# Attention steps of two neighbouring units issued together, and the r-k products in one PSUM bank

## Chip, cores and metric

One core of one Trainium2 chip. The metric is the device time of one execution in microseconds (us); below, times without a unit are in us. The kernel before takes 1027.44 as the median of 3 runs (1026.24 to 1029.26).

## The reference

A decaying linear attention with a state, then two feed-forward layers over all 3072 tokens, all in float32.

```python
# r, k, v, w: (4, 8, 768, 48); u: (8, 48)
for t in range(S):
    cur = np.einsum('bhd,bhe->bhde', u[None] * kt, vt)
    y[:, :, t] = np.einsum('bhd,bhde->bhe', rt, state + cur)
    state = wt[:, :, :, None] * state + np.einsum('bhd,bhe->bhde', kt, vt)
x = y.transpose(0, 2, 1, 3).reshape(3072, 384)
h = x @ w_in                                   # (3072, 2048)
g = np.where(h >= 1, h, np.where(h <= -1, 0.0, (h + 1) ** 2 / 4))
x = g @ w_out                                  # (3072, 384)
g = x @ w_gate; val = x @ w_val                # (3072, 1536) each
out = (g * sigmoid(g) * val) @ w_out2          # (3072, 384)
```

## The kernel before, in words

**Attention** is cut into 24 units: 128 time steps of one batch with its 8 heads. A unit works in two chunks of 64 steps (c = 0, 1) and in four pairs of heads (e = 0, 1 within a pair; the second head of a pair lies from partition 64 on). Fourteen short steps make a unit, each a function `slot_...` with a letter in the table `PLAN`:

- `w`, `i`, `r`, `k`: bring w, r and k into the layout with the head dimension on partitions, make the running products of the decay (G and F), and scale r and k by them. For the first ten units the turning is done by TensorE (four transposes of L234 each, into a bank of PSUM); from unit `UD = 10` on VectorE does it (L217) from data loaded in blocks.
- `a` (`slot_a`, L318): the r-k products, 16 matmuls of 48x64 by 48x64 (L323), for the heads e = 0 and e = 1 in turn; ScalarE copies the two halves out (L332), GpSimd masks them (L333). `n` (L354): four transposes of the scaled k (L359), copied out by ScalarE (L363). `c` (L304): copies of r by ScalarE (L307), r*k*u by GpSimd (L310, L311), the next loads of r and k, and the carried state by VectorE (L289).
- `v` (L338): row sums and their product with v; ScalarE's copies of the carried state (L299). `q` (L366): 16 or 8 matmuls k-v (L373). `s` (L381): the state (L388, L289, L393). `t` (L296): copies by ScalarE (L299).
- `b` (L395): 16 matmuls of 112x64 by 112x48 that give the outputs (L399); VectorE adds (L407); three loads for the unit after next are issued (L185, L179).
- `y` (L416): three transposes of the outputs (L423) and ScalarE's copy `xh` (L426). `x` (L429): VectorE's rest `xl` (L431).

**The feed-forward layers** run as steps (phase, block, i). Phase 1 has 6 blocks of 4 units with 16 steps i each: `front1` is nine matmuls of 128x512 (L521; six with xh, three with xl) followed by ScalarE (L542, L543) and VectorE (L549); `split_act` makes gh (ScalarE L530) and gl (GpSimd L531); `back1` is nine matmuls (L559) of step i-2, since a list `pend` holds two steps back. Nine such matmuls are called a set below. Phase 2 has 6 blocks of 12 steps (L521, L611) and no attention.

**The order of the work** on every engine is the order of the calls (`manual_schedule`). A lead-in list `LEADSEQ` does units 0 to 3 and the beginning of unit 4. After it, time is counted in ticks: unit `un` has its step `nm` at tick `16 * un + PLAN[nm]`. In each step of phase 1, `attn_to` is called twice, once behind `front1` and once behind `back1`, and issues all attention steps whose ticks have come; within a tick they go by unit, and within a unit by a list of letters. Over the 29 calls of one block the ticks advance by 64. The units 4 to 7 are done in block 0, whose x they are for block 1, and so on. So attention stands between sets of feed-forward matmuls, in TensorE's one queue.

**PSUM.** `at_bank` (L226) hands out banks in turn: seven in the lead-in, three afterwards (L719). Of the other five, two are for `front1` and three for `back1`. Whoever gets a bank writes it only when its last reader is done. A unit takes 7 banks (a 2, n 1, q 2, b 1, y 1), and 3 more for w, r and k up to unit 9.

**Weights** arrive as float64. `conv_tick` (L481) turns one chunk of them into two float32r parts with ScalarE (L52 to L54, L495), VectorE (L59, L493, L496) and GpSimd (L489, L496). 9 ticks of it are in the lead-in, 26 in block 0, and two in block 1 that find the queue empty. `open_blk` (L191) then gives the memory of that stage to the block loads of r, k and w.

Of the kernel before, what the change touches and what calls it, by code (L numbers as in the profile page):

```python
# [16 lines left out]
ACTF = mybir.ActivationFunctionType  # L17
# [5 lines left out]
BLOCKS = [4] * 6  # L23

PLAN = {
    "w": 0, "i": 3, "r": 6, "k": 9, "c": 12, "a": 15, "n": 15, "v": 17, "q": 18, "s": 18, "t": 20, "b": 23, "y": 28,
    "x": 30,
}
FILL0 = 5
SKEW = 3  # L30
# [32 lines left out]
def rwkv_ffn_ffn_kernel(  # L63
# [14 lines left out]
    nc = tc.nc  # L78
# [6 lines left out]
    C = 64  # L85
# [5 lines left out]
    NU = NT * B  # L91

    starts = [sum(BLOCKS[:j]) for j in range(len(BLOCKS))]
    blk_of = {s + i: (j, i) for j, s in enumerate(starts) for i in range(BLOCKS[j])}
    NB1 = len(BLOCKS)
# [130 lines left out]
    def at_bank():  # L226
        t = at_b[bn[0] % len(at_b)]
        bn[0] += 1
        return t
# [87 lines left out]

    def slot_a(un):  # L318
        K, R = st[un]["K"], st[un]["R"]
        ab = [at_bank(), at_bank()]  # L320
        for f in range(2 * NP):
            for e in range(2):
                nc.tensor.matmul(  # L323
                    out=ab[e][0:C, f * C:(f + 1) * C],
                    lhsT=K[C * e:C * e + D, f, :],
                    rhs=R[C * e:C * e + D, f, :],
                    start=True,
                    stop=True,
                )
        for e in range(2):  # L330
            At = W[0:C, e]
            nc.scalar.activation(out=At, in_=ab[e][0:C].rearrange("q (f c) -> q f c", c=C), func=ACTF.Copy)  # L332
            nc.gpsimd.affine_select(  # L333
                out=At, in_=At, compare_op=ALU.is_ge, fill=0.0, base=-1,
                pattern=[[0, 2 * NP], [1, C]], channel_multiplier=-1,
            )
# [102 lines left out]
    at_tick = {}  # L439
# [3 lines left out]
    ticks = [0]  # L443
    led = set()

    def tick_of(un):

        return 16 * un + PLAN["x"] + 1

    def attn_to(t):  # L450
        while ticks[0] < t:
            for un, nm in sorted(at_tick.get(ticks[0], []), key=lambda z: (z[0], "wirkcanvqstbyx".index(z[1]))):
                if (un, nm) not in led:
                    stages[nm](un)
            ticks[0] += 1
# [17 lines left out]
    def conv_queue(src, slot, lo_eng):  # L473
        cq.append([src, slot, lo_eng, None])
# [34 lines left out]
    def cols(src, i):  # L509
        return src[:, 2 * i * P:2 * (i + 1) * P]  # L510

    def rows(src, i):
        return src[i * P:(i + 1) * P, :]
# [173 lines left out]
    with tc.manual_schedule():  # L687
        order = [(w_in, i) for i in range(SKEW)]
        for i in range(NF1):
            order += [(w_out, i)] + [(w_in, i + SKEW)] * (i + SKEW < NF1)  # L690
        for c, (src, i) in enumerate(order):
            part, slot = (cols(src, i), ws[2 * i]) if src is w_in else (rows(src, i), ws[2 * i + 1])
            conv_queue(part, slot, nc.vector if c in LOV else nc.gpsimd)
        for what in INIT:
            if what[0] == "n":
                load_nat(int(what[2]), what[1])
            elif what[0] == "v":
                load_v(int(what[1]))
            elif what[0] == "s":
                load_vs(int(what[1]), int(what[2]))  # L700
            elif what[0] == "u":
                nc.sync.dma_start(
                    out=u_b.rearrange("p h d -> p (h d)"), in_=u.rearrange("h d -> (h d)").partition_broadcast(P)
                )
            elif what[0] == "W":
                conv_load(int(what[1]))
        consts()

        for item in LEADSEQ:
            if item == "C":  # L710
                conv_tick()
            elif item[0] == "+":
                keep_warm(int(item))
            else:
                un = int(item[1:])
                stages[item[0]](un)
                led.add((un, item[0]))
        ticks[0] = tick_of(BLOCKS[0] - 1)
        del at_b[3:]  # L719
        pend = []  # L720

        def more_conv(n):
            for _ in range(n):
                conv_tick()

        for n, (ph, j, i) in enumerate(steps):
            if (ph, j, i) == (1, 1, 2):
                open_blk()
            if ph == 1:
                t0 = tick_of(starts[j] + BLOCKS[j] - 1)  # L730
                t1 = tick_of(starts[j + 1] + BLOCKS[j + 1] - 1) if j + 1 < NB1 else t0
            src = (front1 if ph == 1 else front2)(j, i)
            if ph == 1:
                attn_to(min(t1, t0 + (t1 - t0) * (2 * i + 1) // (2 * NF1 - 3)))
                if j == 0 or (j == 1 and i < 2):
                    conv_tick()
            if (ph == 2 and j == 0) or (ph == 1 and j == NB1 - 1 and i > 0):
                more_conv(1)
            if ph == 1 and j == NB1 - 1 and i % 3 == 2:
                more_conv(1)  # L740
            if ph == 1 and j == NB1 - 1 and i in (5, 6, 7):
                split_x1(0, i - 5)
            if ph == 2 and j + 1 < NB2 and i in (6, 7, 8):
                split_x1(j + 1, i - 6)
            if ph == 2 and j in (1, 2) and i % 3 == 2:
                range_check(4 * (j - 1) + i // 3)
            if ph == 1:
                src = gate1(j, src)
            else:
                pend.append((ph, j, i, split_act(src, 512, nc.gpsimd)))  # L750
            if len(pend) > LAG - (ph == 1):
                p_, j_, i_, g_ = pend.pop(0)
                (back1 if p_ == 1 else back2)(j_, i_, g_)
            if ph == 1:
                attn_to(min(t1, t0 + (t1 - t0) * (2 * i + 2) // (2 * NF1 - 3)))
                if j == 0 and (i % 2 == 0 or i < 4):
                    conv_tick()
                pend.append((ph, j, i, split_act(src, BLOCKS[j] * P, nc.gpsimd)))
            if ph == 1 and j == NB1 - 1:
                if i == 0:  # L760
                    open_p2()
                    for c in range(3 * NF2):
                        conv_queue(chunk2(c), slot2(*divmod(c, 3)), (nc.gpsimd, nc.vector)[c % 2])
                    conv_load()
                if i == 1:
                    load_x1(0)
            if ph == 2:
                if j == 0:
                    more_conv(1)
                if j + 1 < NB2:  # L770
                    if i == 2:
                        load_x1(j + 1)
                if j in (1, 2) and i % 3 == 0:
                    range_load(4 * (j - 1) + i // 3)
        for p_, j_, i_, g_ in pend:
            back2(j_, i_, g_)
# [186 lines left out]
```

## Time and profile before

| | |
|---|---|
| median of 3 runs | 1027.44 us |
| profiled execution | 1025.06 us, of which the span from first to last instruction is 1023.1 us |
| busy: TensorE (PE) | 977.9 us, 96% of the span |
| busy: VectorE (DVE), ScalarE (ACT), GpSimd (POOL) | 512.0, 546.2, 464.2 us |
| granted TensorE clock, mean | 0.976 |
| chain that ended last | PE 85%, ACT 5%, DVE 4%, POOL 2% |

The page of the profile lists busy time by engine, 40 slices of the span, the chain that ended last, and groups of instructions by line. Busy time of TensorE counts the pipelined length of a matmul, so two starts are compared below where a duration matters. fp32 products show twice as many matmuls in the trace as the program issues (x32 for 16). In the tables of stretches, block 0 runs from 60.3 to 165.7 us, block 2 from 247.6 to 329.6 us.

### The profile page before, as it was taken

How to read it: one execution, taken by the hardware profiler on the slowest of the kernel's cores; microseconds unless marked ns; L12 is line 12 of the kernel's file. 1: busy time of each engine (PE TensorE's matmuls, PEld its weight loads, DVE VectorE, ACT ScalarE, POOL GpSimd, SP SyncE). 2: the span in 40 equal slices, each digit the busy share in tenths (PEclk: the TensorE clock that was granted, in tenths of full speed). 3: DMA queues.
4: the chain of work that ended last, by engine and by line, in shares of the span. 5: the costliest groups of instructions: out<-in, count | busy, mean ns of one | idle time of the engine just before them, and what ended most of it. 6: DMA issues, size and time to landing. Idle time of an engine off the chain costs nothing.

```text
span 1023.1 us, 16697 instructions
## 1 busy us (share of the span) xinstructions
PE 977.9 (96%) x6430; PEld 817.6 (80%) x6431; DVE 512.0 (50%) x779; ACT 546.2 (53%) x1016; POOL 464.2 (45%) x424
## 2 busy tenths in 40 slices
PE   6678879999999999999999999999999999999997
PEld 4556657888788788788877888888888888888886
DVE  7878866686776777675255663222221222222221
ACT  3678887565656655665699883334333221221211
POOL 4568776544454544454287775232232232232221
PEclk7789989999999999999999999999999999999999
DMA  9755531663455546450443540201200100100000
GB/s 172 168 136 144 142 99 32 161 115 82 109 119 99 121 85 122 98 104 1 130 134 123 178 139 1 85 24 47 86 24 24 62 1 1 62 1 1 31 1 34
DMA packets 164825, 84.33 MB, mean 82 GB/s; under 512 B 115457, under 2 KB 155522, under 8 KB 164738
## 3 DMA queue, kind: packets, MB, share of 16 engines
q1 hardware_dynamic: 164738, 83.19, 33.8%
q8 instruction: 52, 0.85, 0.4%
q14 instruction: 35, 0.29, 0.1%
HBM read 73.73 MB, written 9.44 MB: 81 GB/s over the span
## 4 chain that ended last, share of the span: by engine, by line
PE 85%; ACT 5%; DVE 4%; POOL 2%; issue 2%; SPq 1%; DMA 1%; ACTq 0%; POOLq 0%; DVEq 0%
PE bank L521 45%; PE bank L559 17%; PE bank L611 15%; PE bank L399 2%; PE bank L323 2%; PE bank L359 1%; PE bank L373 1%; DVE ws L496 1%; ACT a L542 1%; POOL t L489 1%; PE bank L234 1%; PE bank L423 1%; DVE F L263 1%; ACT n L53 1%; DVE G L253 1%
## 5 line engine op out<-in xcount | busy, mean ns | idle before, releaser
L531 POOL TENSOR_TENSOR gl<-a,gh 128x512 fp32r<-128x512 f32 x168 | 219.6, 1307 | 440.5 <-ACT gh L530 426.4
L521 PE MATMUL bank<-xh,ws 128*128 128x512 f32 x1332 | 346.7, 396 | 3.5 <-DVE a L549 3.4
L521 PEld LDWEIGHTS bank<-xh,ws 128*128 128x128 f32 x1332 | 246.5, 188 | 54.3 <-DVE a L549 6.0
L530 ACT ACTIVATE gh<-a 128x512 fp32r<-128x512 f32 x168 | 105.5, 628 | 156.7 <-DVE a L601 116.9
L521 PE MATMUL bank<-xl,ws 128*128 128x512 f32 x666 | 188.1, 390 | 0.0
L600 DVE TENSOR_TENSOR a<-a,bank 128x512 f32<-128x512 f32 x72 | 49.5, 687 | 266.5 <-ACT a L599 266.5
L559 PE MATMUL bank<-gh,ws 128*128 128x512 f32 x576 | 153.5, 402 | 0.0
L521 PEld LDWEIGHTS bank<-xl,ws 128*128 128x128 f32 x666 | 125.2, 188 | 27.3
L611 PE MATMUL bank<-ws,gh 128*128 128x384 f32 x528 | 135.0, 336 | 0.0
L599 ACT ACTIVATE a<-bank 128x512 f32<-128x512 f32 x72 | 42.9, 595 | 166.5 <-PE bank L521 166.4
L559 PEld LDWEIGHTS bank<-gh,ws 128*128 128x128 f32 x576 | 104.9, 189 | 22.0 <-ACT x L569 1.1
L542 ACT ACTIVATE a<-bank,half 128x512 f32<-128x512 f32 x96 | 65.5, 682 | 74.0 <-PE bank L521 73.5
L549 DVE SCALAR_TENSOR_TENSOR a<-bank,a 128x512 f32<-128x512 f32 x96 | 65.5, 683 | 71.8 <-ACT a L543 59.7
L611 PEld LDWEIGHTS bank<-ws,gh 128*128 128x128 f32 x528 | 97.0, 188 | 5.0
L611 PE MATMUL bank<-ws,gl 128*128 128x384 f32 x264 | 89.0, 337 | 0.0
L559 PE MATMUL bank<-gl,ws 128*128 128x512 f32 x288 | 81.4, 391 | 0.0
L489 POOL TENSOR_TENSOR t<-t,n 128x384 int32<-128x384 int32 x68 | 76.3, 1124 | 0.4 <-DVE t L59 0.4
L601 DVE TENSOR_TENSOR a<-a,bank 128x512 f32<-128x512 f32 x72 | 49.5, 687 | 44.0 <-PE bank L521 43.3
L559 PEld LDWEIGHTS bank<-gl,ws 128*128 128x128 f32 x288 | 54.0, 188 | 11.8
L543 ACT ACTIVATE a<-a 128x512 f32<-128x512 f32 x96 | 60.7, 632 | 3.1
L59 DVE TENSOR_SCALAR t<-t 128x384 int32<-128x384 int32 x68 | 46.5, 685 | 15.6 <-ACT t L52 15.6
L611 PEld LDWEIGHTS bank<-ws,gl 128*128 128x128 f32 x264 | 49.5, 188 | 0.0
(108 smaller groups left out, 1165.9 us busy)
## 6 DMA issues: line engine op xcount, KB each, us to landing
raw<-in_moe_w_out_dram SPq DMA_DIRECT2D x28, 384.0 KB, 3.7
raw<-in_moe_w_in_dram SPq DMA_DIRECT2D x16, 384.0 KB, 4.2
bw<-in_w_dram SPq DMA_DIRECT2D x56, 96.0 KB, 2.9
br<-in_r_dram SPq DMA_DIRECT2D x56, 96.0 KB, 2.3
bk<-in_k_dram SPq DMA_DIRECT2D x56, 96.0 KB, 3.4
v<-in_v_dram SPq DMA_DIRECT2D x24, 192.0 KB, 3.7
V<-in_v_dram SPq DMA_DIRECT2D x48, 96.0 KB, 3.3
x_d<-x SPq DMA_DIRECT2D x18, 256.0 KB, 2.1
```

What stands on the lines that cost most here:

```text
L59: nc.vector.tensor_scalar(out=t, in0=t, scalar1=3, scalar2=None, op0=ALU.logical_shift_left)
L489: nc.gpsimd.tensor_tensor(out=f, in0=f, in1=three["n"], op=ALU.add)
L521: nc.tensor.matmul(out=bk[:, :n], lhsT=a[:, kk, :], rhs=b[:, kk, :n], start=(i == 0), stop=(i == 3 * KD - 1))
L530: nc.scalar.activation(out=gh[:, :n], in_=src[:, :n], func=ACTF.Copy)
L531: eng.tensor_tensor(out=gl[:, :n], in0=src[:, :n], in1=gh[:, :n].bitcast(F32), op=ALU.subtract)
L542: nc.scalar.activation(out=a[:, :n], in_=bk[:, :n], func=ACTF.Relu, scale=0.5, bias=half)
L543: nc.scalar.activation(out=a[:, :n], in_=a[:, :n], func=ACTF.Square)
L549: nc.vector.scalar_tensor_tensor(out=a[:, :n], in0=bk[:, :n], scalar=1.0, in1=a[:, :n], op0=ALU.max, op1=ALU.min)
L559: nc.tensor.matmul(out=acc_b[m][:, :n], lhsT=a[:, m * P:(m + 1) * P], rhs=b[:, :n], start=(i == 0 and s == 0), stop=(i == NF1 - 1 and s == 2),
L600: nc.vector.tensor_tensor(out=a, in0=a, in1=gb, op=ALU.mult)
L601: nc.vector.tensor_tensor(out=a, in0=a, in1=vb, op=ALU.mult)
L611: nc.tensor.matmul(out=bk[:, :DM], lhsT=a[:, t * P:(t + 1) * P], rhs=slot[:, b], start=(i == 0 and s == 0), stop=(i == NF2 - 1 and s == 2),)
```

## The change

`PLAN` moves steps to later ticks. Of unit un, `b` (tick 31) now falls on the tick of `a` and `n` of unit un+1 (31), and `y` (37) on that of `q` and `s` of unit un+1 (37); `c` comes after `a` and `n`. The r-k products of both heads of a pair go into one bank, those of e = 1 to partitions 64 to 127. A unit now takes 6 banks (9 up to unit 9). The ticks of block 0 go from 79 to 151 (72 of them; they went from 79 to 143), in the same 29 calls; the other blocks keep 64. `open_blk` is called two steps sooner, and the two empty ticks of `conv_tick` are gone. `LEADSEQ` is the same.

```diff
 PLAN = {
-    "w": 0, "i": 3, "r": 6, "k": 9, "c": 12, "a": 15, "n": 15, "v": 17, "q": 18, "s": 18, "t": 20, "b": 23, "y": 28,
-    "x": 30,
+    "w": 0, "i": 3, "r": 6, "k": 9, "a": 15, "n": 15, "c": 16, "v": 19, "q": 21, "s": 21, "t": 23, "b": 31, "y": 37,
+    "x": 38,
 }
...
-        ab = [at_bank(), at_bank()]
+        ps = at_bank()
...
-                    out=ab[e][0:C, f * C:(f + 1) * C],
+                    out=ps[C * e:C * (e + 1), f * C:(f + 1) * C],
...
-            nc.scalar.activation(out=At, in_=ab[e][0:C].rearrange("q (f c) -> q f c", c=C), func=ACTF.Copy)
+            nc.scalar.activation(out=At, in_=ps[C * e:C * (e + 1)].rearrange("q (f c) -> q f c", c=C), func=ACTF.Copy)
...
-        ticks[0] = tick_of(BLOCKS[0] - 1)
+        ticks[0] = 16 * BLOCKS[0] + PLAN["a"]
+        first = ticks[0]
...
-            if (ph, j, i) == (1, 1, 2):
+            if (ph, j, i) == (1, 1, 0):
                 open_blk()
             if ph == 1:
-                t0 = tick_of(starts[j] + BLOCKS[j] - 1)
-                t1 = tick_of(starts[j + 1] + BLOCKS[j + 1] - 1) if j + 1 < NB1 else t0
+                t0 = tick_of(starts[j] + BLOCKS[j] - 1) if j else first
+                t1 = tick_of(starts[j + 1] + BLOCKS[j + 1] - 1) if j + 1 < NB1 else tick_of(NU - 1)
...
-                if j == 0 or (j == 1 and i < 2):
+                if j == 0:
                     conv_tick()
```

The place in each block where outputs and r-k products stand, on TensorE. Before, in block 1 (L399 outputs, L423 their transposes, L323 r-k products, L359 transposes of k; bank_94 to bank_96 are attention's three):

```order
L399 MATMUL bank_96<-V_1_154,W 64x48
...
L521 MATMUL bank_92<-xh,ws_116 128x512 x6
L521 MATMUL bank_92<-xl,ws_116 128x512 x3
...
L423 MATMUL bank_94<-ident,rk 128x128 x3
L521 MATMUL bank_93<-xh,ws_118 128x512 x6
L521 MATMUL bank_93<-xl,ws_118 128x512 x3
L323 MATMUL bank_95<-F_148,K 64x64
L323 MATMUL bank_96<-F_148,K 64x64
...
L359 MATMUL bank_94<-ident,K 128x128 x4
L559 MATMUL bank_89<-gh,ws_115 128x512
```

Now, in block 1 as well:

```order
L521 MATMUL bank_92<-xl,ws_108 128x512 x3
L399 MATMUL bank_95<-V_0_153,W 64x48
...
L323 MATMUL bank_96<-F_149,K 64x64 x16
L359 MATMUL bank_94<-ident,K 128x128 x4
L559 MATMUL bank_89<-gh,ws_105 128x512
...
L521 MATMUL bank_93<-xl,ws_110 128x512 x3
L423 MATMUL bank_95<-ident,rk 128x128 x3
L373 MATMUL bank_96<-v,kt 48x48
L373 MATMUL bank_94<-v,kt 48x48
```

The outputs of one unit stand directly ahead of the r-k products of the next, and the transposes of the outputs directly ahead of the next unit's k-v products; each was a group between two sets of its own.

The same engine in block 0, where r, k and w are still turned by TensorE (L234; nr and nw are r and w). Before, the transposes of k take the bank of L423, and those of w one of the two banks of L323:

```order
L423 MATMUL bank_95<-ident,rk 128x128 x3
L559 MATMUL bank_89<-gh,ws_107 128x512
...
L323 MATMUL bank_96<-F_149,K 64x64
L323 MATMUL bank_94<-F_149,K 64x64
...
L359 MATMUL bank_95<-ident,K 128x128 x4
L521 MATMUL bank_92<-xh,ws_112 128x512 x6
L521 MATMUL bank_92<-xl,ws_112 128x512 x3
L234 MATMUL bank_96<-ident,nw_136 128x128 x4
```

Now:

```order
L423 MATMUL bank_96<-ident,rk 128x128 x3
L373 MATMUL bank_94<-v,kt 48x48
L373 MATMUL bank_95<-v,kt 48x48
...
L234 MATMUL bank_96<-ident,nr_138 128x128 x4
L521 MATMUL bank_93<-xh,ws_114 128x512 x6
```

The bank of L423 is next taken by the transposes of r, which stand behind the k-v products in the same group.

## Rows read from the trace of the kernel before

**Rows 1.** Stretches: length, busy (x count) of PE, PEld, DVE, ACT, POOL; clock, DMA share, GB/s.

```profile
60.30:165.70 105.40, 89.89 (x732) 69.91 (x731) 79.28 (x124) 88.92 (x177) 81.55 (x75) 0.95 0.49 127
247.60:329.60 82.00, 82.00 (x702) 65.79 (x701) 60.64 (x88) 50.51 (x91) 38.62 (x37) 1.00 0.51 107
```

**Rows 2.** Waits of PE: total us, times, longest; two of block 0, one from 170 us on.

```profile
PE bank L234 <- ACT W L332: 7.7, 3, 6.4
PE bank L359 <- DVE xl L431: 5.2, 2, 4.0
...
PE bank L521 <- DVE a L549: 2.4, 2, 1.7
```

**Rows 3.** Timeline of PE, block 2: start, length, line, operation; a and n, then q.

```profile
250.89 0.84 PE L521 MATMUL bank<-xl,ws 128*128 128x512 f32 x3
251.66 1.15 PE L323 MATMUL bank<-F,K 48*64 48x64 f32 x32
252.74 0.66 PE L359 MATMUL bank<-ident,K 128*128 128x128 f32 x4
...
254.62 0.86 PE L559 MATMUL bank<-gl,ws 128*128 128x512 f32 x3
255.41 0.58 PE L373 MATMUL bank<-v,kt 64*48 64x48 f32 x32
...
257.41 0.84 PE L521 MATMUL bank<-xl,ws 128*128 128x512 f32 x3
...
259.45 0.84 PE L559 MATMUL bank<-gl,ws 128*128 128x512 f32 x3
```

**Rows 4.** Timeline of PE, block 2: outputs b between two sets.

```profile
280.04 0.84 PE L559 MATMUL bank<-gl,ws 128*128 128x512 f32 x3
280.81 1.14 PE L399 MATMUL bank<-V,W 112*64 112x48 f32 x32
281.88 1.66 PE L521 MATMUL bank<-xh,ws 128*128 128x512 f32 x6
283.37 0.84 PE L521 MATMUL bank<-xl,ws 128*128 128x512 f32 x3
```

**Rows 5.** Timeline of PE, lead-in at the low clock: b directly ahead of a.

```profile
40.43 2.11 PE L399 MATMUL bank<-V,W 112*64 112x48 f32 x30 [3.41 <-ACT V L299]
42.47 1.97 PE L323 MATMUL bank<-F,K 48*64 48x64 f32 x32
```

**Rows 6.** Timeline of PE, block 0: transposes of r directly ahead of b.

```profile
121.31 0.85 PE L521 MATMUL bank<-xl,ws 128*128 128x512 f32 x3
122.00 0.60 PE L234 MATMUL bank<-ident,nr 128*128 128x128 f32 x4
122.52 1.14 PE L399 MATMUL bank<-V,W 112*64 112x48 f32 x32
...
125.08 0.85 PE L559 MATMUL bank<-gl,ws 128*128 128x512 f32 x3
```

**Rows 7.** Timeline, block 0: from the transposes y to the transposes of k.

```profile
78.96 0.50 PE L423 MATMUL bank<-ident,rk 128*128 128x128 f32 x3
...
85.41 0.47 ACT L426 ACTIVATE xh<-bank 128x384 fp32r<-128x384 f32 x1
...
86.75 1.11 PE L359 MATMUL bank<-ident,K 128*128 128x128 f32 x4 [3.98 <-DVE xl L431]
...
87.52 2.80 PE L521 MATMUL bank<-xh,ws 128*128 128x512 f32 x6
```

**Rows 8.** ACT's groups in block 0: busy us, mean ns, idle before.

```profile
L299 ACT ACTIVATE V<-m 48x192 f32<-48x192 f32 x16 | 5.8, 362 | 2.5 <-DVE m L289 2.2
L332 ACT ACTIVATE W<-bank 64x512 f32<-64x512 f32 x8 | 4.2, 576 | 0.0
L363 ACT ACTIVATE kt<-bank 128x384 f32<-128x384 f32 x4 | 1.9, 476 | 0.0
```

**Rows 9.** DMA issues of b's loads on the page: KB each, us to landing.

```profile
V<-in_v_dram SPq DMA_DIRECT2D x48, 96.0 KB, 3.3
```

More of the change, by code (lines that the diff above doesn't have):

```diff
@@ L451, in attn_to @@
         while ticks[0] < t:
-            for un, nm in sorted(at_tick.get(ticks[0], []), key=lambda z: (z[0], "wirkcanvqstbyx".index(z[1]))):
+            for un, nm in sorted(at_tick.get(ticks[0], []), key=lambda z: (z[0], "wirkancvqstbyx".index(z[1]))):
                 if (un, nm) not in led:
```

## The prediction

> **What bounds the kernel now.** I read the busy shares, then the table of stretches, then TensorE's waits, and last its timeline. The stretches show two kinds of time. In block 2 TensorE is busy for all of 82.00 us, while ScalarE has 50.51, VectorE 60.64 and GpSimd 38.62 [rows 1]; from 170 us to the end of attention it has no wait to speak of [rows 2]. There the time is the sum of what stands in TensorE's queue. Block 0 is different: of 105.40 us TensorE is busy 89.89, and the clock granted is 0.95; ScalarE is busy 88.92, the other two about 80 [rows 1], because the weights are converted there. Of the 15.5 us in which TensorE stands, 12.9 are two waits for a bank of attention: the transposes of w for ScalarE's copies of the r-k products (7.7), and those of k for the rest xl of the outputs (5.2) [rows 2]. The longest take 6.4 and 4.0. So a saving on TensorE counts in full behind block 0, and in block 0 the question is who waits for whom.
>
> **Prices on TensorE.** I compare the start of the last three matmuls of one set with that of the next set. With nothing between them this is 2.04 (257.41 to 259.45) [rows 3], or 0.227 a matmul. With a and n between them it is 3.73, so they cost 1.69; with q 2.79, so q costs 0.75 [rows 3]. With b it is 3.33, so b costs 1.29 [rows 4]. That 1.29 has three parts: 0.09 until it begins (0.77 less three matmuls, 0.68), 1.07 from its first product to the next set, and 0.13 by which the six first matmuls of that set are slow (1.49 for 1.36) [rows 4]. Products a also begin 0.09 late [rows 3].
>
> **Part 1: b directly ahead of a and n.** The restart of a set behind b (0.13) and the entry of a (0.09) go, if the step from b to a costs no more than that from b to a set. The lead-in shows that step at the low clock: 2.04 for 15 pairs of products and the step, 0.136 a pair [rows 5], against 1.07 for 16 pairs and the step to a set, 0.067 a pair, at the full clock [rows 4]. Twice the time at half the clock: the steps cost the same. So a join saves 0.22. Bounds: nothing, if the step eats it, and 0.31, if b's own 0.09 went too. There are 19 joins, 4 in block 0 and 15 behind it: 15 x 0.22 = **3.3 us** (0 to 4.7).
>
> **Part 2: y directly ahead of q.** Nearest row: transposes of r directly ahead of b. The two cost 3.77 - 2.04 = 1.73, that is b's 1.29 and 0.44 for four transposes [rows 6], 0.11 each, which is what a 128x128 transpose takes in the stream. Transposes and sets have the same shape on the array, so there was nothing to leave or enter in front of y, and the entry into q stays. I take 0 (0 to 0.09 each, the entry of a small product, 1.4 in all).
>
> **Part 3: eight ticks more in block 0.** Counted from the tables, block 0 takes over from later blocks a and n of unit 8, its q, and the transposes of w and r of unit 9: 1.69 + 0.75 + 2 x 0.44 = **3.3 us** less behind block 0. The last block gets no substitute.
>
> **Part 4: block 0 itself.** TensorE has 15.5 us free there, so its own 3.3 more is no price by itself. ScalarE has the longest work: unit 8 adds two copies L332, one L363 and two L299, 2 x 0.58 + 0.48 + 2 x 0.36 = 2.4 [rows 8]. If the engines hinder one another as much as before, the block gets 2.4 longer. The waits change places. The wait of k's transposes for xl goes: they now take the bank that k itself was read from, which a needs anyway. The wait of w for the copies L332 goes: its bank is now b's, read by VectorE. New is that the transposes of r take the bank of y, three times in the same group (behind q of units 5, 7 and 8), once a set later. They wait for ScalarE's xh and VectorE's xl. ScalarE ran late in this block: xh came 6.4 after y's transposes began [rows 7], and k's transposes could go 7.8 after them. So a new wait is at most 7.8 - 0.3 (y) - 0.75 (q) = 6.7, and, ScalarE being prompt, at least the 1.3 from xh's start to the release of the bank (85.41 to 86.75) [rows 7]; since VectorE has the three steps of s to do before xl, which wait for q (0.75), I call it 2. Three times 2 to 6.7 is 6 to 20, against the 12.9 that go. I take them as equal, for ScalarE's work sets the pace. After the 4.0 wait the next six matmuls took 2.80 [rows 7] where 1.66 is usual [rows 4], at the lower of the two clock levels; with shorter and more even waits I count one of the two such restarts as gone, 1.1. Block 0: 2.4 - 1.1 = **1.3 us longer** (from 5 shorter to 9 longer: waits of 2 or 6.7, 3.3 of work absorbed or not, both slow restarts gone or none).
>
> **Costed at nothing.** The products of a in one bank: 16 matmuls as before, still in pairs for e = 0 and e = 1; first and last pair start the same way. ScalarE's two copies read 64 partitions each as before. Clustered evacuation: where b, a, n and c fall into one call, ScalarE has the two L332, L363 and c's copies in a row ahead of gh, and GpSimd masks and multiplies ahead of gl. Since `back1` runs two steps behind, three sets (6.1) lie between the burst and the use of that gh; the delay is at most the burst, 1.29 + 1.69, and the 1.6 of L332 and L363, 4.6. If that cover were gone, some 1 or 2 us would be due at one place in each of four blocks. Queues: b's three loads leave 8 ticks later, about 10 us by 82.0 for 64 ticks [rows 1]; v is used 20 ticks (25 us) on and V 32, with 3.3 to landing [rows 9]. c's loads of r and k leave 4 ticks later and have 16 ticks. The block loads open two steps sooner, behind the last conversion, which stands in step 15 of block 0; GpSimd's three fills and SyncE's twelve issues wait there for nothing new. The lead-in has the same order and needs fewer banks: 0.
>
> **Sum.** 1025.06 (the profiled execution, span 1023.1) - 3.3 - 3.3 + 1.3 = 1019.8. The median is 2.38 above the profiled execution, so **1022.1** as a median. What 0.3% is, about all that a measurement here can tell from no change, is 3.1 us; the forecast is 5.3 faster.
>
> **A rule against the sum.** In the trace the pairs of a run two at a time: 16 pairs in 1.08 (251.66 to 252.74) [rows 3], with the two halves on different partitions of the input and in two banks. No row has two row halves of the array writing one bank at once; q, which does use all four quarters, sends each row half to a bank of its own. The Trainium skill, page "TensorEngine Tiling (Array Packing)", section Restrictions and Gotchas, says that different row tiles cannot access the same PSUM bank simultaneously. By that rule a's two halves would have to take turns; the sum above would be some 20 us higher.
>
> **Rivals.**
> - *The bank holds the halves apart (slower).* The mechanism is in a: pairs that shared 0.067 take turns, 1.08 becomes up to 2.16. 20 units behind the lead-in give up to 21.6, a part of the five in block 0 hidden: about 19, so 1041. It decides from the point where a is 0.27 longer, a quarter of its 1.08, since 20 x 0.27 is the whole 5.3. For it: the halves never shared a bank. Against it: b's pairs share one bank on different output partitions at 1.07 for 16 pairs [rows 4]; but there the halves are of columns. Chance 0.08.
> - *Block 0 eats it (no change).* The transposes of r meet a late ScalarE each time: 3 x 6.7 = 20 for 12.9, and the 3.3 of work is not absorbed. Block 0 grows by about 9; 1027.4 - 6.6 + 9 = 1030; with waits of 5 it is 1025. For it: xh was 6.4 late [rows 7]. Against it: TensorE's standing lets ScalarE catch up. Chance 0.17.
> - *Joining saves nothing.* The step from b to a drains like two. 1022.1 + 3.3 = 1025.4. For it: r ahead of b saved nothing [rows 6]. Against it: the lead-in's step. Chance 0.13.
> - *Block 0 gains.* The new waits are short (2 each) and the clock stays up: block 0 is 5 shorter, 1015.8. Chance 0.10.
>
> **How the numbers follow.** The forecast itself gets 0.45, with 1018 to 1024.3 of its own; 0.07 is left for what I don't see, mostly late gh and gl. Faster by over 0.3% (below 1024.4): 0.45 + 0.10 + 0.04 of the joins + 0.02 = 0.61. Within it: 0.09 of the joins + 0.11 of block 0 + 0.02 = 0.22. Slower (above 1030.5): 0.06 + 0.08 + 0.03 = 0.17. The range takes in the gain in block 0 with the upper bound of the joins (1014) and block 0 at its worst (1031); it leaves out the bank rival.
>
> **What would show it.** In the profile after: block 2 at about 81.1 instead of 82.0, and block 4 shorter by 3 or more; b, a and n between two sets at 2.76 (1.29 + 1.69 - 0.22); 16 pairs of a still in about 1.08; y and q together at about 1.1. In block 0: no wait of L359 for xl, none of L234 for L332, but L234 (nr) waiting for xl, two to four times. Wrong: a near 2 us; waits of L559 for gh or gl in blocks 1 to 4; a block 0 over 112 or under 99.

## The result, and where the time went

The changed kernel takes 1038.45 us as the median of 4 runs (1037.6 to 1039.22), beside 1027.47 for the kernel before: ratio 1.0109, 95% interval [1.0096, 1.0121]. It is slower by 11 us where 5 faster was forecast. The profiled execution took 1038.19, its span is 1036.2, the mean granted clock 0.972. All stretches, waits and timelines below come from one such execution of each kernel, while the executions of one kernel differ by up to 5 (1024.97 to 1029.77 in e11).

The table of stretches for the kernel after, blocks 0 to 4 (length, busy of PE, PEld, DVE, ACT, POOL, clock, DMA share, GB/s):

```profile
61.00:187.10 126.10, 96.41 (x808) 78.42 (x807) 87.86 (x133) 93.23 (x182) 87.96 (x78) 0.86 0.41 104
187.10:268.20 81.10, 81.10 (x705) 66.72 (x705) 59.88 (x87) 49.17 (x89) 44.40 (x39) 1.00 0.51 114
268.20:348.80 80.60, 80.60 (x702) 66.34 (x700) 62.40 (x88) 50.74 (x92) 44.61 (x36) 1.00 0.50 109
348.80:429.40 80.60, 80.60 (x686) 66.44 (x685) 61.78 (x87) 51.19 (x92) 44.57 (x36) 1.00 0.49 110
429.40:507.80 78.40, 78.40 (x586) 64.51 (x585) 44.90 (x61) 48.67 (x87) 37.04 (x32) 1.00 0.29 74
```

The same for the kernel before, blocks 1 and 4; blocks 0 and 2 are in [rows 1], and block 3 is as long as block 2:

```profile
165.80:249.60 83.80, 83.49 (x714) 67.14 (x713) 56.86 (x86) 51.75 (x94) 41.01 (x41) 1.00 0.49 105
...
413.70:495.70 82.00, 82.00 (x638) 65.84 (x637) 49.93 (x73) 49.33 (x89) 36.48 (x34) 1.00 0.34 77
```

Behind block 0 the change gains: block 1 is 2.7 shorter, blocks 2 and 3 are 1.4 shorter each and block 4 is 3.6 shorter, 9.1 in all. Block 0 loses 20.7 (105.40 to 126.10). The lead-in is 0.7 longer (61.00 for 60.30) and what follows block 4 1.0 longer, which I did not follow up. In block 0 TensorE stands for 29.7 (126.10 less 96.41) instead of 15.5, and is busy 6.5 longer: 3.3 of that, by the prediction's prices, is the work of eight more ticks, and the rest goes with the clock of 0.86 (it was 0.95). TensorE's waits in block 0 after the change (in total, times, longest) show where:

```profile
PE bank L234 <- DVE xl L431: 26.5, 4, 10.6
PE bank L234 <- DVE S L388: 1.8, 1, 1.8
```

The two waits of before [rows 2] are gone, as forecast, and four new ones have come, one at r of each of the units 6 to 9. (The wait for L388 is one more: k's transposes now take the first bank of q, which VectorE frees with the state.) The first in TensorE's timeline after:

```profile
85.34 0.60 PE L234 MATMUL bank<-ident,nw 128*128 128x128 f32 x4
...
89.91 0.49 PE L423 MATMUL bank<-ident,rk 128*128 128x128 f32 x3
90.33 0.58 PE L373 MATMUL bank<-v,kt 64*48 64x48 f32 x32
101.47 1.11 PE L234 MATMUL bank<-ident,nr 128*128 128x128 f32 x4 [10.57 <-DVE xl L431]
102.23 2.91 PE L521 MATMUL bank<-xh,ws 128*128 128x512 f32 x6
```

From the transposes of w (85.34) to those of r TensorE has two sets, y and q; it is done with them at 90.9 and stands for 10.57. The six matmuls after it run at the low clock level (granted clock 0.50), 2.91 for the usual 1.66 [rows 4]; so they do after each of the four (2.81 to 2.91), and after the wait for L388 (2.91). Meanwhile VectorE's timeline after has no idle time:

```profile
86.97 0.67 DVE L245 TENSOR_SCALAR F<-bank 128x512 f32<-128x512 f32 x1
...
87.67 3.88 DVE L253 TENSOR_TENSOR_SCAN G<-F,seed 128x520 f32<-128x520 f32 x1
91.48 1.09 DVE L59 TENSOR_SCALAR t<-t 128x384 int32<-128x384 int32 x1
92.49 1.35 DVE L496 TENSOR_TENSOR ws<-t,ws 128x384 fp32r<-128x384 f32 x1
...
94.45 1.61 DVE L263 TENSOR_TENSOR_SCAN F<-F,seed 128x520 f32<-128x520 f32 x1
...
99.75 0.34 DVE L388 TENSOR_TENSOR S<-bank,m 112x192 f32<-112x192 f32 x1
...
100.87 0.55 DVE L431 TENSOR_TENSOR xl<-bank,xh 128x384 fp32r<-128x384 f32 x1
```

This is the thing to see. Between VectorE's reading of w (L245, 86.97) and xl (100.87), which frees the bank that r wants, stand both scans of the decay of unit 6, whose r it is, five instructions of weight conversion (5.7), the row sums, a step of the feed-forward layer (L549) and the state, 13.2 in all. VectorE does them in the order of the program. In the kernel before, r's transposes took the bank of w, whose last reader is L245, ahead of all that.

VectorE is not the only late one. xl needs ScalarE's xh, and xh is late too. From the timelines of ScalarE and VectorE after, xh and xl of the four units (xl of the first is above):

```profile
96.27 0.46 ACT L426 ACTIVATE xh<-bank 128x384 fp32r<-128x384 f32 x1
...
124.04 0.46 ACT L426 ACTIVATE xh<-bank 128x384 fp32r<-128x384 f32 x1
126.51 0.55 DVE L431 TENSOR_TENSOR xl<-bank,xh 128x384 fp32r<-128x384 f32 x1
...
151.13 0.47 ACT L426 ACTIVATE xh<-bank 128x384 fp32r<-128x384 f32 x1
152.38 0.55 DVE L431 TENSOR_TENSOR xl<-bank,xh 128x384 fp32r<-128x384 f32 x1
...
174.82 0.47 ACT L426 ACTIVATE xh<-bank 128x384 fp32r<-128x384 f32 x1
177.12 0.55 DVE L431 TENSOR_TENSOR xl<-bank,xh 128x384 fp32r<-128x384 f32 x1
```

xh begins 6.4, 4.4, 5.1 and 3.8 behind y's transposes, and xl follows it by 4.6, 2.5, 1.3 and 2.3. Where VectorE was ready and stood for xh, xl followed by 0.5 (146.52 and 147.02 in the trace of e9), and r's transposes begin 0.6 behind xl. So, as an estimate from these rows with ScalarE's times as they are, the four waits would be 6.5, 2.2, 5.2 and 3.9 if VectorE had nothing ahead of xl: some 18 of the 26.5 go with xh, and VectorE's queue adds 8.6.

In the steady part the prices are as forecast. TensorE's timeline after, block 1, b with a and n, then y with q:

```profile
251.51 0.84 PE L559 MATMUL bank<-gl,ws 128*128 128x512 f32 x3
252.28 1.14 PE L399 MATMUL bank<-V,W 112*64 112x48 f32 x32
253.35 1.15 PE L323 MATMUL bank<-F,K 48*64 48x64 f32 x32
254.43 0.66 PE L359 MATMUL bank<-ident,K 128*128 128x128 f32 x4
...
256.31 0.86 PE L521 MATMUL bank<-xl,ws 128*128 128x512 f32 x3
...
260.41 0.84 PE L521 MATMUL bank<-xl,ws 128*128 128x512 f32 x3
261.09 0.49 PE L423 MATMUL bank<-ident,rk 128*128 128x128 f32 x3
261.51 0.57 PE L373 MATMUL bank<-v,kt 64*48 64x48 f32 x32
...
263.51 0.84 PE L559 MATMUL bank<-gl,ws 128*128 128x512 f32 x3
```

Set to set the first burst takes 4.80 (251.51 to 256.31), so b, a and n cost 4.80 - 2.04 = 2.76, and y with q 3.10 - 2.04 = 1.06. In the kernel before, y alone stood like this:

```profile
285.41 0.85 PE L559 MATMUL bank<-gl,ws 128*128 128x512 f32 x3
286.10 0.49 PE L423 MATMUL bank<-ident,rk 128*128 128x128 f32 x3
...
287.82 0.84 PE L521 MATMUL bank<-xl,ws 128*128 128x512 f32 x3
```

That is 2.41 - 2.04 = 0.37; with q's 0.75 it makes 1.12. So the second join saves 0.06 and the first 0.22: 1.1 a block of four units, of the 1.4 by which blocks 2 and 3 are shorter; the other 0.3 is not explained.

### The profile page after: what moved, and what is told of

Same layout as the page of the kernel before. It is cut to its first block, busy times and chain, and to the rows that moved or that the text cites. A ratio compares the mean times of both kernels' runs of the same rounds, so it can differ in the third digit from the quotient of the medians.

```text
span 1036.2 us, 16614 instructions
## 1 busy us (share of the span) xinstructions
PE 979.6 (95%) x6431; PEld 828.1 (80%) x6431; DVE 521.0 (50%) x779; ACT 549.7 (53%) x1016; POOL 486.0 (47%) x424
## 4 chain that ended last, share of the span: by engine, by line
PE 87%; DVE 7%; ACT 3%; SPq 1%; issue 1%; DMA 0%; POOL 0%; DVEq 0%; ACTq 0%
PE bank L521 46%; PE bank L559 18%; PE bank L611 15%; PE bank L399 3%; PE bank L323 2%; DVE F L263 1%; DVE G L253 1%; PE bank L359 1%; PE bank L234 1%; PE bank L373 1%; DVE ws L496 1%; DVE t L59 1%; PE bank L423 1%; DVE m L289 1%; DMA ew<-in_w_dram 0%
## 5 line engine op out<-in xcount | busy, mean ns | idle before, releaser
L531 POOL TENSOR_TENSOR gl<-a,gh 128x512 fp32r<-128x512 f32 x168 | 238.4, 1419 | 423.1 <-ACT gh L530 421.8
L530 ACT ACTIVATE gh<-a 128x512 fp32r<-128x512 f32 x168 | 105.4, 627 | 181.0 <-DVE a L601 117.1
L559 PE MATMUL bank<-gh,ws 128*128 128x512 f32 x576 | 154.6, 405 | 0.0
L559 PEld LDWEIGHTS bank<-gh,ws 128*128 128x128 f32 x576 | 109.2, 194 | 22.5 <-ACT x L569 0.3
L549 DVE SCALAR_TENSOR_TENSOR a<-bank,a 128x512 f32<-128x512 f32 x96 | 65.6, 683 | 71.6 <-ACT a L543 66.2
L559 PE MATMUL bank<-gl,ws 128*128 128x512 f32 x288 | 82.4, 395 | 0.0
L489 POOL TENSOR_TENSOR t<-t,n 128x384 int32<-128x384 int32 x68 | 73.8, 1088 | 5.4 <-DVE t L59 5.4
L559 PEld LDWEIGHTS bank<-gl,ws 128*128 128x128 f32 x288 | 55.3, 192 | 12.0
L333 POOL TENSOR_SCALAR_AFFINE_SELECT W<-W 64x512 f32<-64x512 f32 x48 | 36.7, 785 | 42.7 <-ACT W L332 42.7
L59 DVE TENSOR_SCALAR t<-t 128x384 int32<-128x384 int32 x68 | 44.7, 659 | 12.3 <-ACT t L52 12.3
```

Source lines behind the costliest of these rows:

```text
L59: nc.vector.tensor_scalar(out=t, in0=t, scalar1=3, scalar2=None, op0=ALU.logical_shift_left)
L489: nc.gpsimd.tensor_tensor(out=f, in0=f, in1=three["n"], op=ALU.add)
L530: nc.scalar.activation(out=gh[:, :n], in_=src[:, :n], func=ACTF.Copy)
L531: eng.tensor_tensor(out=gl[:, :n], in0=src[:, :n], in1=gh[:, :n].bitcast(F32), op=ALU.subtract)
L549: nc.vector.scalar_tensor_tensor(out=a[:, :n], in0=bk[:, :n], scalar=1.0, in1=a[:, :n], op0=ALU.max, op1=ALU.min)
L559: nc.tensor.matmul(out=acc_b[m][:, :n], lhsT=a[:, m * P:(m + 1) * P], rhs=b[:, :n], start=(i == 0 and s == 0), stop=(i == NF1 - 1 and s == 2),
```

## The experiments

Three theories were on record at the start: T1, the transposes of r wait for the bank of y; T2, VectorE has too much to do in block 0; T3, the two halves of a hold each other up in one bank. T4 came later. The kernel before took 1026.7 to 1027.0 as the median beside the experiments. Block 0 is 105.4 before and 126.1 after.

**The one bank.** e3 gives the changed kernel two banks for a again; e4 gives the kernel before one bank and nothing else.

```diff
-        ps = at_bank()
+        ab = [at_bank(), at_bank()]
...
-                    out=ps[C * e:C * (e + 1), f * C:(f + 1) * C],
+                    out=ab[e][0:C, f * C:(f + 1) * C],
```

> The changed kernel with the r-k products in two banks as before. Theory 1: the banks go round by ten a unit in block 0, the transposes of r still take the bank of y, and those of k now that of the outputs b: 1036 to 1046. Theory 2: 1034 to 1042. Theory 3: back to 1027 or below.

> The kernel before with the r-k products in one bank, and nothing else of the change. Theories 1 and 2: behind block 0 nothing changes (a stays at 1.08); in block 0 the transposes of w now take the bank of y, and the waits of k for xl and of w for L332 give way to one for xl: 1020 to 1030. Theory 3: a is longer by up to 1.08 in each of 24 units: 1040 to 1050.

Measured: e3 1041.3, ratio 1.013 [1.0112, 1.0148], block 0 126.1 as in the changed kernel; e4 1027.38, ratio 1.0005 [0.9996, 1.0015]. T3 falls: one bank costs nothing alone. In the joined burst it is even needed: with two banks the turn of the banks now and then gives n the bank of b just ahead of it, as TensorE's timeline of e3 shows:

```profile
298.89 1.14 PE L399 MATMUL bank<-V,W 112*64 112x48 f32 x32
299.96 1.15 PE L323 MATMUL bank<-F,K 48*64 48x64 f32 x32
302.13 0.66 PE L359 MATMUL bank<-ident,K 128*128 128x128 f32 x4 [1.02 <-DVE rk L407]
```

**y behind r** (e1: r takes w's bank again, y and x apart from q).

```diff
-... "b": 31, "y": 37, "x": 38,
+... "b": 31, "y": 40, "x": 41,
```

> The changed kernel with the steps y and x at ticks 40 and 41, behind the transposes of r and not ahead of them. Theory 1 (the bank: in block 0 TensorE stands because the transposes of r take the bank that y holds until VectorE's late xl): the four waits of L234 for xl, 26.4 us together, go, block 0 falls from 126.1 to between 100 and 112, and the run takes 1012 to 1024. Theory 2 (the load: VectorE has too much to do in block 0, with 72 ticks for 64 and scans stretched beside GpSimd): TensorE stands elsewhere, block 0 stays over 120 and the run over 1032. Theory 3 (the two halves of a in one bank hold each other up): nothing changes, 1036 to 1040.

Measured: 1032.07, ratio 1.0057 [1.004, 1.0074]. Its block 0 and the largest, in total, of its waits there:

```profile
60.60:174.00 113.40, 92.00 (x813) 72.60 (x812) 90.51 (x136) 94.72 (x185) 86.45 (x79) 0.97 0.46 117
```

```profile
PE bank L423 <- DVE S L388: 5.9, 3, 2.6
```

Block 0 is 12.7 shorter, although it holds three ticks more, and its clock is back at 0.97. TensorE still stands 21.4 in it, but in fourteen small pieces, of which the longest is 2.9. The block is just above the 100 to 112 of T1 and well below the 120 of T2; the time is 8 above T1's range, in part because the blocks behind are longer (block 1 is 82.8 for 81.1, with a wait of 1.7 for ScalarE's copy L569). So the bank matters, and it is not all.

**Block 0 as before** (e2: units 0 to 7 by the old table, the others by the new).

```diff
+PLAN0 = {... "c": 12, "a": 15, "n": 15, "v": 17, "q": 18, "s": 18, "t": 20, "b": 23, "y": 28, "x": 30}
...
-        for nm, off in PLAN.items():
+        for nm, off in (PLAN0 if un < 8 else PLAN).items():
...
-        return 16 * un + PLAN["x"] + 1
+        return 16 * un + (PLAN0 if un < 8 else PLAN)["x"] + 1
```

> The changed kernel with the old ticks for units 0 to 7, so that block 0 has the order of before (with the r-k products in one bank) and the new order begins with unit 8. Theories 1 and 2: block 0 back at 98 to 108, and behind it the 15 joins give 3.3 us: 1018 to 1025. Theory 3: still slower than before, over 1035.

Measured: 1024.41, ratio 0.9972 [0.9962, 0.9981], the lowest median of this study (its interval overlaps those of e12 and e14 below). Block 0 is 105.1, blocks 2 to 4 are as in the changed kernel (80.7, 80.6, 78.4), and block 1, which now has the eight extra ticks, is 87.6. So the whole loss of the change lies in how block 0 is ordered and filled.

**Which bank, or VectorE as a whole?** e5 puts q ahead of y within the tick, so that r takes a bank that VectorE frees with the state L388; e7 leaves out VectorE's shifts L59 in block 0, a part of the conversion of the weights.

```diff
-key=lambda z: (z[0], "wirkancvqstbyx".index(z[1]))
+key=lambda z: (z[0] + (z[1] == "y"), "wirkancvqstbyx".index(z[1]))
```

> The changed kernel, with the k-v products q of the next unit ahead of the transposes y within their tick. In block 0 the transposes of r then take q's first bank, which VectorE frees with the state (L388), and y's bank goes to the outputs b, some ten ticks later. T1 (the bank of y, with its late reader xl, is the cause): the long waits go, as when y stood behind r; block 0 at 113 to 116, time 1026 to 1032. T2 (VectorE is some 10 us late, whichever bank is asked for): in the trace of the changed kernel L388 stands only 1.1 us ahead of xl in VectorE's queue (99.75 against 100.87), so the same four waits now name L388 and are about 1 us shorter each; block 0 at 119 to 126, time 1032 to 1038.

```diff
-        if two:
+        if two and not 8 <= two["c"] < 32:
             shift3(nc, two["t"])
```

> The changed kernel without VectorE's shifts L59 of the 24 chunks of weights that are converted in block 0; that leaves out part of the conversion of the weights. It takes some 17 us (24 by 0.73) off VectorE's 87.9 in block 0 and nothing else. T2 (VectorE is late by its load): it catches up between the units, the waits for xl fall from 26.5 to below 13, block 0 to 104 to 115; time 1016 to 1028. T1 in the form in which I predicted it (ScalarE's xh sets when the bank of y is free: 96.27 for transposes at 89.91): the waits stay at 5 to 6 each, 20 or more in all; time 1031 to 1036.

Measured: e5 1032.0, ratio 1.0043 [1.0027, 1.006], block 0 119.7. The time lies where its two forecasts meet; the block, and the four waits, each 1.4 to 2.1 shorter, are nearer to T2. The waits now name the state:

```profile
PE bank L234 <- DVE S L388: 21.1, 5, 9.1
```

So it was not xl as such: any bank freed from that part of VectorE's queue will do, and no xh of ScalarE is in this wait. That looked like T2, but e7 speaks against T2: 1033.9, ratio 1.0068 [1.0051, 1.0085], where T2 wanted 1028 or less and T1, with ScalarE's xh as the bound, 1031 to 1036. VectorE is busy 72.61 in block 0 instead of 87.86, block 0 is only 3.5 shorter, and TensorE waits nearly as long as ever:

```profile
60.70:183.30 122.60, 95.54 (x808) 77.26 (x807) 72.61 (x112) 93.90 (x184) 86.72 (x78) 0.87 0.44 109
```

```profile
PE bank L234 <- DVE xl L431: 24.3, 4, 10.8
```

15 us less work on VectorE took 2.2 off these waits, so the sum of its work does not set them. Only what stands ahead of xl counts: of the shifts left out, 7.5 stood between the readings of w and xl in the four units, and these stretches got 3.8 shorter (42.3 to 38.5), since VectorE now stands 3.3 in them for ScalarE and GpSimd. ScalarE's xh, which my prediction had as the bound, is not cleared by this: T1 expected waits of 20 or more with it and they are 24.3, and xh still begins 7.9, 4.4, 4.7 and 2.7 behind y's transposes. e5 and e7 together say that two queues are late by nearly as much: r waits 19.2 in e5 with no xh in it (21.1 with k's wait), and by the estimate above some 18 are left without VectorE's queue. Relieving one of the two shows little.

**The order of VectorE's queue (T4).** e9 keeps all work and moves only i (L261 and the scan L263) behind s and xl.

```diff
-    "w": 0, "i": 3, "r": 6, ...
+    "w": 0, "i": 6, "r": 6, ...
```

> The changed kernel with i (the reciprocal L261 and the scan L263 of r's scaling) at tick 6, directly ahead of r's product L272, instead of tick 3. VectorE's work is the same; only the order in its queue changes: 1.8 us of i now stand behind s and xl of the unit before, not ahead of them. T4 (new, since taking 17 us of load off VectorE left the waits as they were: the bank that r's transposes take is freed by an instruction that stands behind both scans in VectorE's queue, and it is the length of that piece of queue which TensorE waits for): each of the four waits gets about 1.8 shorter, 26.5 in all becomes 17 to 21; block 0 at 116 to 121, time 1028 to 1034. T2 (the sum of work on the other engines): nothing is gained, 1036 to 1040.

Measured: 1031.08, ratio 1.0042 [1.0028, 1.0056], block 0 118.9. The waits:

```profile
PE bank L234 <- DVE xl L431: 22.0, 4, 9.5
```

With the same work in another order each wait is 0.7 to 1.8 shorter, 4.5 together (expected were 5.5 to 9.5), the wait of 1.8 for L388 is gone, and the kernel gains 7: more than by taking 15 us of load away. In the changed kernel i took 7.4 of the four stretches ahead of xl, and these got 4.9 shorter; VectorE now stands 6.2 in them for ScalarE and GpSimd, and two of the four waits end with xh. In the first stretch the scan L253 also took 1.56 for 3.88, so the 1.1 gained there is not i's alone. e11 does the same to e1.

> The kernel of e1 (y, x at ticks 40, 41, behind r) with i at tick 6. In e1 the remaining waits of block 0 name VectorE's state (L388, L393) for y and k: 11.0 in all; the state now stands ahead of i's 1.8 us. T4: these waits fall to 6 or less, block 0 from 113.4 to 106 to 110, time 1024 to 1029. If something else paces block 0: as e1, 1030 to 1034.

Measured: 1027.07, ratio 0.9998 [0.9988, 1.0008], block 0 107.6. The waits for L388 and L393 fell from 11.0 to 5.2. The two orders together, r's bank and i's place, bring block 0 from 126.1 to 107.6, 2.2 above the kernel before, with more ticks in it.

**The order in a kernel without the change.** e13 is the kernel before with one bank (as e4) and y late, so that r takes y's bank; b is not joined with a. (The expectation says that nothing is joined, but y at tick 34 falls on the tick of the next unit's q, 16 + 18, and stands directly ahead of it: 91.44 and 91.95 in TensorE's timeline.)

```diff
-... "b": 23, "y": 28, "x": 30,
+... "b": 23, "y": 34, "x": 36,
```

> The kernel before with the r-k products in one bank (which alone changed nothing, e4) and y, x of all units at ticks 34, 36, with block 0 ending at tick 149 for it; b, q, c as before, nothing joined. In block 0 the transposes of r then take the bank of y, as in the changed kernel, four ticks (1.6 sets) behind it, and xl stands behind both scans in VectorE's queue. T4: TensorE's waits name L234 for xl three or four times, 3 to 6 each; block 0 at 113 to 120, time 1031 to 1040. If the joined bursts or c's place are needed for the loss: block 0 at 105 to 110, time 1025 to 1030.

Measured: 1051.81, ratio 1.025 [1.0235, 1.0264]. Block 0 is 117.8, for 106.6 in e4, and its largest wait is the one foretold, though uneven: 8.0, 3.3 and 2.8 where 3 to 6 each were expected:

```profile
PE bank L234 <- DVE xl L431: 14.1, 3, 8.0
```

So this order makes the wait by itself, though c stands at its old place and b is apart from a (block 0 has six ticks more than e4's, which is part of the 11). Here xl begins 5.9, 4.3 and 5.3 behind xh, so it is VectorE's queue that sets the end of all three. The time is above the range: from block 1 on other waits came (the outputs b, 10.9 in all), which I did not expect and did not pursue.

**Better orders.** e12 has e11's order for units 0 to 7 alone, e14 besides c one tick sooner, e10 y behind k for all units, e8 has e2 with a longer way from n to q.

```diff
+PLAN0 = dict(PLAN, i=6, y=40, x=41)
```

> The changed kernel with i at tick 6 and y, x at ticks 40, 41 for units 0 to 7 only; the other units by the changed table, y with q again. T4 (the loss is the order of r's bank and VectorE's queue in block 0, nothing else): block 0 as with this order for all units, 107 to 109; blocks 2 to 4 as in the changed kernel (80.6, 80.6, 78.4), block 1 at 81 to 84; together 1020 to 1025, below both kernels. If the joins cost something that the order hid (a late gh or gl, a burst at the edge of a block): 1026 or more.

> The kernel of e12 with c of units 0 to 7 at tick 15, behind a and n of the same tick, instead of 16, so that the loads of the next unit's r and k leave one tick (some 0.8 us) sooner. In the kernel of e11 r's transposes waited for those loads 0.7 to 1.1, three times. If that is worth its time: 1 to 3 below e12. If the waits only move to the state (L388, L393): within 1 of e12.

> The changed kernel with i at tick 6 and y, x at ticks 42, 43, behind k of the next unit. r's transposes then take the bank of w, freed ahead of the scans, as before the change; k takes q's first bank three ticks later, y q's second one, and y's own bank goes to n, five ticks on. T4 (which bank, and what stands ahead of its reader): no wait above 2 in block 0, block 0 at 103 to 110, time 1019 to 1027, although block 0 holds 77 ticks of attention and y, x are apart from q again (about 1 us a block). If ScalarE's work paces block 0 however the banks turn (94.7 busy where y stood behind r): block 0 at 111 to 116, 1027 to 1033.

> The kernel of e2 (units 0 to 7 by the old ticks, the others by the new) with v, q, s, t and b of units 0 to 7 one or two ticks later (19, 20, 20, 22, 24). In e2 TensorE waits 8.5 us in block 0 with q for ScalarE's copy kt (longest 6.0). T2 (other engines' lateness makes the waits; a longer way between the steps hides it): half or more of the 8.5 goes, time 1019 to 1023. If the wait only moves to the next step that needs ScalarE (b waits for V, L403 for L299): 1023 to 1026.

Measured: e12 1025.08, just above its range, ratio 0.9987 [0.9979, 0.9996], with blocks 1 to 4 of 83.1, 80.7, 80.7 and 78.4 as expected and a block 0 of 111.1, 2 above its range; the last paragraph of the next section finds out why. e14 1024.89, ratio 0.9986 [0.9978, 0.9995]: no difference from e12, so a tick of c is worth nothing here. In e10 block 0 is 106.0, in its range, but the kernel takes 1047.51, ratio 1.0189 [1.0172, 1.0206]: T4 was right of block 0 (but for a wait of 2.8, where none above 2 was expected) and I had missed what happens behind it:

```profile
PE bank L559 <- ACT x L569: 20.5, 4, 5.6
```

Four times, about once a block, ScalarE's copy of the last block's results is late by some 5; ScalarE stands there for the store of an earlier result (23.5 in all in e10's trace). e8 takes 1025.54, ratio 0.999 [0.9981, 1.0]: the wait of q for kt is gone and b waits for V in its place, 8.3 in all, as its second alternative said.

**c at its old place** (e6). At tick 12, c of one unit comes ahead of b of the unit before, so b reads the next unit's copies of r.

```diff
-    "w": 0, "i": 3, "r": 6, "k": 9, "a": 15, "n": 15, "c": 16, ...
+    "w": 0, "i": 3, "r": 6, "k": 9, "c": 12, "a": 15, "n": 15, ...
```

> The changed kernel with c (ScalarE's copies of r, GpSimd's r*k*u) back at tick 12, ahead of a and n, as before the change; all else as changed. T2 with the scan as the main load (c now falls on the tick of the next unit's w, and VectorE's scan L253 is stretched beside GpSimd's L310 and L311, 2.56 us in the mean against 1.42 before): the scans go back to about 1.5, VectorE has 5 us less in block 0, the waits for xl go from 26.5 to 15 to 22; time 1029 to 1035. T1 (the bank; the stretched scan is a side show that other work of GpSimd would cause as well): the waits stay within 3 us of 26.5; 1035.5 to 1040.

Measured: 1042.97, ratio 1.0155 [1.0138, 1.0172], block 0 126.5. Neither forecast of the time held. The scans L253 fell to 2.01 in the mean and the waits for xl to 19.6, inside the 15 to 22 of T2, but b now waited for c's copies (L307), 5.0 in block 0. With two causes in it, this run settles nothing.

## Why the prediction was wrong

**Part 1 held.** The join of b with a and n saves 0.22 (2.76 for 1.29 + 1.69). **Part 2** gave 0.06 a unit, inside its bounds. **Part 3**: block 4 is 2.2 and block 1 1.3 shorter beyond the 1.4 of blocks 2 and 3; that 3.5 is the work that went into block 0, forecast at 3.3. Behind block 0 the gain is 9.1 where 6.6 was forecast; the parts make 3.3, 0.9 and 3.5, and 1.4 is not explained. **Costed at nothing** held too, for what it named: no wait of L559 for gh or gl in blocks 1 to 4, and the pairs of a take 1.08 in one bank (253.35 to 254.43). The rule of the Trainium skill, page "TensorEngine Tiling (Array Packing)", section Restrictions and Gotchas, that was weighed against the sum, does not show here: two row halves that write different partitions of one bank go on in pairs, in e4 too (253.74 to 254.82).

**Part 4 failed**: block 0 is 20.7 longer where 1.3 (-5 to 9) was forecast. The step that failed is "a new wait is at most 7.8 - 0.3 (y) - 0.75 (q) = 6.7 ... I take them as equal, for ScalarE's work sets the pace". That r would wait for xl was right, and that the two old waits would go. But I set the new waits at the 12.9 of the old ones, and they are 26.5 for r and 1.8 for k, which I had not seen. ScalarE was read rightly: xh came 6.4 behind y once more, and its part alone, 18 by the estimate above, is over the 12.9, in part because I priced three waits of the four and the one a set later was 4.2 all the same. What I left out is VectorE's queue, the other 8.6, which took the first wait to 10.6, over the bound of 6.7; the others are under it. That bound was carried over from [rows 7], where y stands elsewhere: there no scan was left ahead of xl when y's transposes began. In the new order xl has both of unit 6 ahead of it (L253 at 87.67, L263 at 94.45), and the conversions between them. I looked for the late engine, found ScalarE, and did not read what now stood ahead of xl in VectorE's queue; the order of the instructions, which needs no run, would have shown it. e5 (19.2 of waits for r with no xh in them) and e13 show that this queue alone can hold r; how the 26.5 divide between the two engines is the estimate and no run. With block 0 as it was before, the joins are worth what was forecast for them, some 3 us (e2).

Two smaller steps of Part 4 failed with it. "TensorE has 15.5 us free there, so its own 3.3 more is no price by itself": it stands 14.2 longer and is busy 6.5 longer as well, so nothing was absorbed. And I counted one of two slow restarts as gone, where there are five, each some 1.25 (2.91 for 1.66).

**The rivals.** "Block 0 eats it" had the right place and the right kind of wait, but with ScalarE's price it ended at 1030. "The bank holds the halves apart", the one rival on the slower side, fell with e3 and e4. "Joining saves nothing" and "Block 0 gains" fell with the rows above.

**What e12 adds, and what stays open.** Block 0 of e12 is 111.1 and that of e11 107.6, with the same order on TensorE in it. The order on VectorE is not the same: units 8 and 9 are scaled in block 0 and keep i at tick 3 in e12. There the scan of unit 8 (L264, which is L263 in the other kernels) stands ahead of the state (L389, else L388) that frees the bank y wants. TensorE's timeline of e11, then VectorE's and TensorE's of e12:

```profile
140.44 0.55 PE L423 MATMUL bank<-ident,rk 128*128 128x128 f32 x3 [0.74 <-DVE S L388]
```

```profile
138.18 1.86 DVE L264 TENSOR_TENSOR_SCAN F<-F,seed 128x520 f32<-128x520 f32 x1
...
141.83 0.34 DVE L389 TENSOR_TENSOR S<-bank,m 112x192 f32<-112x192 f32 x1
```

```profile
142.23 0.55 PE L424 MATMUL bank<-ident,rk 128*128 128x128 f32 x3 [2.88 <-DVE S L389]
```

y waits 2.1 longer here and 0.8 longer at unit 9 (1.44 for 0.66), k's next wait is 0.75 shorter, and the six matmuls behind it run at a granted clock of 0.54, 2.80 for 1.63. Together that is 3.3 of the 3.5: two units with the old place of i, and the same kind of wait. Open are the 1.4 behind block 0 and the waits of e13 from block 1 on.

## What to carry to other kernels

When buffers are handed out in turn, moving one step changes who waits for whom: list for each taker the last reader of its buffer, and then everything that stands ahead of that reader in its engine's queue, the next unit's long instructions above all. Where a buffer has two late readers on two engines, relieving one of them shows little (e7). The wait shrinks by moving the taker (e1, e11) or by moving what stands ahead of the reader (e9); work that stands elsewhere in that engine's queue hardly matters. And a bound for a wait is only good for the order in which it was measured.

## What was unexpected of the hardware

VectorE's scan L253 took 3.88 in the stretch shown above, and the same scan of the same unit 1.56 in e9, where other work of GpSimd lay beside it. (The spans of GpSimd in a profile are rough.) GpSimd's timeline after, beside the 3.88 (87.67 to 91.55):

```profile
87.50 1.01 POOL L489 TENSOR_TENSOR t<-t,n 128x384 int32<-128x384 int32 x1
88.48 1.01 POOL L496 TENSOR_TENSOR ws<-t,ws 128x384 fp32r<-128x384 f32 x1
89.45 1.00 POOL L310 TENSOR_TENSOR rk<-nr,nk 128x384 f32<-128x384 f32 x1
90.53 1.82 POOL L311 TENSOR_TENSOR rk<-rk,u_b 128x384 f32<-128x384 f32 x1
```

Three products of GpSimd follow one another until 90.45; from there to the end of the scan are 1.1, about what it takes undisturbed (1.24 for L263 in e9), and the fourth product, which began meanwhile, took 1.82 for 1.00. It looks as if the scan had stood for three instructions, and the fourth for the scan; in e9 it is the product L489 that took 1.93 beside the scan. The Trainium skill, page "SBUF — State Buffer", section "SBUF: two separate sides", says that a VectorE operation with two inputs in SBUF and a GpSimd operation that reads SBUF exclude each other for a whole instruction. These rows agree, and they suggest that VectorE can lose several turns running. Over block 0 the five scans L253 took 12.8 after the change, for 7.1 before. How much of the 26.5 of waits this made is open, since the run meant to tell it (e6) was confounded.
